# Block means of the values in the lead: value rows as weights under four streaming columns, then a turn by the identity

## The chip, the cores and the metric

The kernel runs on 1 core of one Trainium2 chip. The metric is the time of one execution on the device in microseconds, lower is better. TensorE (PE for its matmuls, PEld for its weight loads), VectorE (DVE), ScalarE (ACT), GpSimd (POOL) and the queue of the DMA issues on SyncE (SP) run side by side, each in the order of its own program.

## The reference

An attention with a band of neighbours and block summaries feeds two feed-forward layers. What matters here is the attention: each query sees the keys nearer than 16 and, for each block of 32 positions, one summary key (the maximum) and one summary value (the mean).

```python
B, H, S, D = q.shape            # 2, 8, 768, 64
block, window = (32, 16)
k_sum = k.reshape(B, H, nb, block, D).max(axis=3)
v_sum = v.reshape(B, H, nb, block, D).mean(axis=3)
scores_l = scale * np.matmul(q, k.transpose(0, 1, 3, 2))
mask_l = np.abs(pos[:, None] - pos[None, :]) < window
scores_s = scale * np.einsum('bhsd,bhnd->bhsn', q, k_sum) + np.log(block)
a = softmax(concatenate([where(mask_l, scores_l, -1e9), scores_s]))
attn = np.matmul(a, np.concatenate([v, v_sum], axis=2))
x = attn, 1536 tokens x 512
x = (relu(x @ w_in) ** 2) @ w_out             # 512 -> 2048 -> 512
x = silu(x @ w_in2) @ w_out2
```

The change touches how `v_sum` of the first batch is computed: 24 means (`NSUM`) of 32 value rows each, for all 512 columns.

## The kernel before

The 1536 tokens are worked off in 24 attention tiles of 64 queries (`QT`). A tile sees 96 neighbour positions (`NWIN`) and the 24 summaries: 120 keys (`NK`), with 4 pairs of heads (`NHP`). The first layer runs in three blocks of 512 tokens, the second layer after them. The first 8 tiles (`NLEAD`) are the lead: they must be done before the first feed-forward product `h0_0` can start. The matmuls of the layers use fp32r operands split in high and low parts; those of the attention are fp32, and each fp32 matmul stands in the trace as two records, each with a weight load of its own. The PE transposes (`psa`, `psv1`) are one record each.

For a lead tile the steps are: `psl` (scores `pss`, one pair of heads at a time, in quarters of the array), `ttl` on DVE (mask and minimum), `exl` on ACT (exponential into `T`), `ze`, `rc`, `nt` on DVE (sum, inverse, norm), `psa` on PE (L480, four transposes of T), `a` (copy to SBUF, on DVE for tiles 5, 6 and 7, else on ACT), and for two tiles together `av` (L503, products with the values), `xh` on ACT and `xl` on DVE (high and low parts of the layer's input `xt0`).

The means of the values: `share` (L376 to L397) holds a pattern of 1/32. `vs(c)` (L709) is one matmul for each 128 value rows, six in all, with a slice of `share` as weights (24 columns) and 512 value columns streaming; they add up in the PSUM tile `psv0` on partitions 96 to 119. `vmean(i)` (L713) is an ACT copy that spreads `psv0` over four tiles' value operands (`vlead`), i = 0 for tiles 0 to 3 and i = 1 for 4 to 7. `av` reads `vlead`.

What sets the order: `first_order()` (L70) lists every step of the first block with an engine, a duration, a due time and its dependencies, plays them through, and the program is recorded in the resulting order, engine by engine (L831 to L834). The engines then run in just that order. In the first block that fixes PE, DVE, ACT and the DMA issues of SP. The table's durations and due times are the author's; a due time decides between steps that are ready together. The weight chunks of the layers are decoded in the same order by ACT (`sc`: `c_wi`, `c_wo`; `hi`: `wi`, `wo`) and DVE (`sh`, `st2`, `lo`).

Of the kernel before, what the change touches and what calls it, by code (L numbers as in the profile page):

```python
# [10 lines left out]
F32 = mybir.dt.float32  # L11
# [8 lines left out]
B, H, S, D = 2, 8, 768, 64  # L20
DM, DFF = 512, 2048
NTOK = B * S
P = 128
WIN = 16
KBLK = 32
NSUM = S // KBLK
QT = 64
NWIN = QT + 2 * WIN
NK = NWIN + NSUM
TPB = S // QT  # L30
NG = B * TPB
NHP = H // 2
# [12 lines left out]
NLEAD = 8  # L45
NGRP = 4
# [3 lines left out]
PHASE = 96  # L50
# [19 lines left out]
def first_order():  # L70
# [3 lines left out]
    A, M = .15, .25  # L74
    shift = dict()

    def op(eng, name, arg, dur, due, deps=(), bank=(), kb=0):
        o = index[name, arg] = dict(eng=eng, name=name, arg=arg, dur=dur, due=due + shift.get(name, 0), deps=list(deps), bank=bank, kb=kb,
                                    n=len(ops))
        ops.append(o)  # L80
# [27 lines left out]
            op("act", "kwl", (hp, i), .5, -50 + hp + 51 * i, [("kt", hp, 0)])  # L108
            op("vec", "ksl", (hp, i), .13, -50 + hp + 48 * i, [("ksum", hp, 0)])
    for c in range(6):  # L110
        op("pe", "vs", c, .92, 2.7 + .1 * c, [("vr", c // 2, 0)])
    for i in range(NLEAD // NGRP):
        op("act", "vmean", i, 1.9, -5, [("vs", c, M) for c in range(6)] + [("vl", i, 0)] * 0)
    for i in range(NVF):
        op("act", "vfm", i, .6, tile_due(NLEAD) - 10 + i, [("vmean", 0, 0), ("xh", LEADX[-1], 0)])

# [107 lines left out]
    while todo:  # L224
# [5 lines left out]
        t, _, _, o = min(picks)  # L230
        t, _, _, o = min((p for p in picks if p[3]["eng"] == o["eng"] and p[0] <= t), key=lambda p: p[1:3])
# [13 lines left out]
def kernel(  # L245
# [17 lines left out]
    vec, act, pool, pe, sp = nc.vector, nc.scalar, nc.gpsimd, nc.tensor, nc.sync  # L263
# [10 lines left out]
    ps_h = ctx.enter_context(tc.tile_pool(name="ps_h", bufs=2, space=PSUM))  # L274
# [3 lines left out]
    def mm(o, l, r, **kw):  # L278
        pe.matmul(o, l, r, **kw)  # L279

    def copy(eng, o, i, scale=1.0):
        if eng is act:
            return act.activation(out=o, in_=i, func=AF.Copy, scale=scale)  # L283
        return eng.tensor_copy(out=o, in_=i)  # L284
# [88 lines left out]


    share_p = ctx.enter_context(tc.tile_pool(name="share_p", bufs=1, side="right"))
    share = share_p.tile([P, PHASE - 8], F32, tag="share", name="share")  # L376
    att_ctx = ExitStack()
    cp = att_ctx.enter_context(tc.tile_pool(name="cp", bufs=1, side="right"))
    p1 = att_ctx.enter_context(tc.tile_pool(name="p1", bufs=1, side="right"))
# [2 lines left out]
    first_p = first_ctx.enter_context(tc.tile_pool(name="first_p", bufs=1))  # L382

    cst_sb = cp.tile([P, 8 * LINE], F32, tag="cst", name="cst_sb")
    id_sb = cst_sb[:, 3 * NK:3 * NK + P]
# [7 lines left out]
    ksum, vsum, vsumT = {}, {}, {}  # L393

    pool.memset(share, 0.0)
    for j in range(P // KBLK):
        pool.memset(share[j * KBLK:(j + 1) * KBLK, NSUM - P // KBLK + j:NSUM - P // KBLK + j + 1], 1.0 / KBLK)  # L397
    st = {}

    def summaries(b, sums, tag):  # L400
# [234 lines left out]
    def first_block():  # L635
        x = xt[0]
        ws, kts, vrows, hs, gs, rs, cs, halves = {}, {}, {}, {}, {}, {}, {}, {}
# [1 line left out]

        idle_in = wi_p.tile([P, 512], F32R, tag="wi", name="idle_in")  # L640
        idle_out = ps_h.tile([P, 512], F32, tag="h", name="idle_out")
        psv = ps_h.tile([P, DM], F32, tag="h", name="psv0")
        vec.memset(idle_in.bitcast(F32), 0.0)
        early = first_p.tile([P, 1], F32, tag="early", name="early")
        act.activation(out=early, in_=idle_in[:, 0:1].bitcast(F32), func=AF.Exp)
# [61 lines left out]
            turn(FILL.get(ghp, 0))  # L707

        def vs(c):  # L709
            lo = NSUM - P // KBLK - c * (P // KBLK)  # L710
            mm(psv[NWIN:NK], share[:, lo:lo + NSUM], vrows[c // 2][:, c % 2], start=(c == 0), stop=(c == S // P - 1))

        def vmean(i):  # L713
            means = psv[NWIN:NK]
            copy(act, vlead[NWIN:NK, i * NGRP:i * NGRP + NGRP].rearrange("p g h d -> p g (h d)"),
                 bass.AP(means.tensor, means.offset, [means.ap[0], [0, NGRP], means.ap[1]]))

# [101 lines left out]
        def psa(g):  # L819
            for i in (g,) if g < NLEAD else (g, g + 1):  # L820
                transposes(i)

        do = dict(kt=kt, q=q, cst=cst_, vr=vr, vl=vl, ksum=ksum_, kwl=kwl, ksl=ksl, vs=vs, vmean=vmean, vfm=vfm, kv=kv, kvr=kvr,
                  vend=vend, vendc=vendc, vfc=vfc, kw=kw_load, qr=q_load, vf=v_load, kwc=k_sums, qd=side_by_side,
                  vis=vis, ttr=minima, exp=exps, ze=guard, rc=inverse, psl=psl, ttl=lambda a: minimum(*a),
                  exl=lambda a: exponential(*a), nt=lambda g: norm(g, vec),
# [2 lines left out]
                  st2=lambda xs: dec_join(name(xs), cs[xs]), scr=scr_, hi=hi, lo=lo, highs=highs, gemm1=gemm1_, relu=relu, sq=sq, gh=gh,  # L829
                  gl=gl, gemm2=gemm2_)  # L830
        steps = first_order()  # L831
        steps.remove(("gemm2", NF - 1))
        for what, arg in steps:
# [56 lines left out]
    with tc.manual_schedule(engines={e.engine for e in (vec, act, pe, sp)}):  # L890
        rest = first_block()
# [64 lines left out]
    us, vs = {}, {}  # L956
# [263 lines left out]
```

## Time and profile before

| what | value |
|---|---|
| median of 3 runs | 583.91 us (583.61 to 584.04) |
| the profiled execution's own time | 583.73 us |
| its span in the profile | 581.9 us |
| PE busy | 574.5 us, 99% |
| ACT busy | 360.1 us, 62% |
| DVE busy | 386.4 us, 66% |
| lead, up to the first record of `h` | 34.9 us |

The span counts from the first to the last instruction of the profiled execution; 1.8 us of its own time lie around it. Busy time of PE counts overlapping records once and includes the drain of a pipelined matmul; how close the records follow one another is read from the chain of waits, which gives each stretch the time until its successor could go on.

### The profile page before, as it was taken

How to read it: one execution, taken by the hardware profiler on the slowest of the kernel's cores; microseconds unless marked ns; L12 is line 12 of the kernel's file. 1: busy time of each engine (PE TensorE's matmuls, PEld its weight loads, DVE VectorE, ACT ScalarE, POOL GpSimd, SP SyncE). 2: the span in 40 equal slices, each digit the busy share in tenths (PEclk: the TensorE clock that was granted, in tenths of full speed). 3: DMA queues.
4: the chain of work that ended last, by engine and by line, in shares of the span. 5: the costliest groups of instructions: out<-in, count | busy, mean ns of one | idle time of the engine just before them, and what ended most of it. 6: DMA issues, size and time to landing. Idle time of an engine off the chain costs nothing.

```text
span 581.9 us, 9507 instructions
## 1 busy us (share of the span) xinstructions
PE 574.5 (99%) x3300; PEld 489.5 (84%) x3300; DVE 386.4 (66%) x966; ACT 360.1 (62%) x834; POOL 93.0 (16%) x101
## 2 busy tenths in 40 slices
PE   8999999999999999999999999999999999999997
PEld 6578888888888888888888889999988988889995
DVE  5999899953955765286454778666665666666641
ACT  5999878864646545376544677565555655555541
POOL 0010100102654452175332200000000000000000
PEclk9999999999999999999999999999999999999999
DMA  8999989755998879345880111242258411111002
GB/s 317 310 267 330 316 296 333 241 212 168 295 339 289 298 245 364 122 134 160 313 262 2 38 54 73 90 146 90 91 169 338 146 37 37 36 37 37 27 12 108
DMA packets 42240, 104.42 MB, mean 179 GB/s; under 512 B 4560, under 2 KB 11856, under 8 KB 42192
## 3 DMA queue, kind: packets, MB, share of 16 engines
q1 hardware_dynamic: 42192, 103.81, 52.7%
q8 instruction: 26, 0.43, 0.3%
q14 instruction: 22, 0.18, 0.1%
HBM read 78.37 MB, written 25.43 MB: 178 GB/s over the span
## 4 chain that ended last, share of the span: by engine, by line
PE 96%; ACT 2%; DMA 1%; DVE 1%; SPq 0%; issue 0%; DVEq 0%
PE acc L279 45%; PE h L279 23%; PE hx L279 12%; PE hz L279 6%; PE pss L279 3%; PE hy L279 3%; PE psa L483 2%; PE av L279 1%; DMA t_ksum<-in_kT_dram 1%; PE psv L279 1%; ACT vlead L283 1%; ACT T L446 0%; ACT xt L283 0%; PE idle_out L279 0%; DVE ksum L684 0%; DVE T L441 0%
## 5 line engine op out<-in xcount | busy, mean ns | idle before, releaser
L279 PE MATMUL h<-xt,wi 128*128 128x512 f32 x576 | 139.8, 392 | 1.0 <-ACT xt L283 1.0
L279 PE MATMUL acc<-g,wo 128*128 128x512 f32 x576 | 139.5, 391 | 0.0
L279 PE MATMUL acc<-wq,g 128*128 128x512 f32 x576 | 134.3, 390 | 0.0
L279 PEld LDWEIGHTS h<-xt,wi 128*128 128x128 f32 x576 | 107.1, 188 | 23.9 <-ACT xt L283 1.1
L279 PEld LDWEIGHTS acc<-g,wo 128*128 128x128 f32 x576 | 107.6, 188 | 22.6 <-issue 0.5
L279 PEld LDWEIGHTS acc<-wq,g 128*128 128x128 f32 x576 | 107.8, 188 | 21.9 <-DVE wq L287 0.3
L287 DVE TENSOR_TENSOR g<-r,g 128x512 fp32r<-128x512 f32 x48 | 38.8, 807 | 66.0 <-ACT g L283 40.1
L287 DVE TENSOR_TENSOR r_s<-v,r_s 128x256 fp32r<-128x256 f32 x48 | 20.3, 426 | 64.7 <-ACT r_s L283 64.7
L283 ACT ACTIVATE e<-hx 128x384 f32<-128x384 f32 x32 | 15.7, 492 | 60.4 <-PE hx L279 60.4
L446 ACT ACTIVATE T<-T,m 128x120 f32<-128x120 f32 x96 | 36.6, 382 | 7.0 <-DVE m L441 6.9
L283 ACT ACTIVATE g<-s 128x384 fp32r<-128x384 f32 x64 | 32.9, 516 | 10.5 <-DVE s L287 10.4
L279 PE MATMUL hx<-x_t,r_s 128*128 128x384 f32 x192 | 38.5, 335 | 0.0
L287 DVE TENSOR_TENSOR g<-s,g 128x384 fp32r<-128x384 f32 x64 | 35.3, 555 | 2.7 <-ACT g L283 1.1
L279 PEld LDWEIGHTS hx<-x_t,r_s 128*128 128x128 f32 x192 | 33.8, 188 | 0.3
L1032 ACT ACTIVATE s<-e 128x384 f32<-128x384 f32 x48 | 25.1, 523 | 8.4 <-DVE e L287 7.1
L284 POOL COPY qd<-qr 128x256 f32<-128x256 f32 x16 | 12.0, 767 | 111.0 <-PE pss L279 68.2
L287 POOL TENSOR_TENSOR wo<-c_wo,wo 128x512 fp32r<-128x512 f32 x16 | 25.9, 1619 | 19.2 <-ACT wo L283 18.7
L588 ACT ACTIVATE r<-h 128x512 f32<-128x512 f32 x16 | 9.6, 597 | 30.9 <-PE h L279 30.9
L592 ACT ACTIVATE r<-h 128x512 f32<-128x512 f32 x16 | 9.5, 593 | 30.6 <-PE h L279 30.6
L287 DVE TENSOR_TENSOR s<-e,s 128x384 f32<-128x384 f32 x48 | 26.4, 551 | 0.3 <-ACT s L1032 0.3
L287 POOL TENSOR_TENSOR r<-r 128x512 f32<-128x512 f32 x16 | 16.6, 1040 | 49.3 <-ACT g L593 38.1
L477 DVE TENSOR_SCALAR T<-T,r 128x120 f32<-128x120 f32 x96 | 24.2, 316 | 0.5
(112 smaller groups left out, 905.8 us busy)
## 6 DMA issues: line engine op xcount, KB each, us to landing
raw_wi<-in_w_in_dram SPq DMA_DIRECT2D x16, 512.0 KB, 5.0
raw_wo<-in_w_out_dram SPq DMA_DIRECT2D x16, 512.0 KB, 5.4
raw_wp<-in_w_out_dram SPq DMA_DIRECT2D x16, 512.0 KB, 4.9
split<-wo SPq DMA_DIRECT2D x16, 512.0 KB, 3.8
raw_wj<-in_w_in_dram SPq DMA_DIRECT2D x16, 512.0 KB, 4.7
wo<-split SPq DMA_DIRECT2D x16, 512.0 KB, 3.6
c<-scr_dram SPq DMA_DIRECT2D x32, 256.0 KB, 2.8
scr_dram<-c_wo SPq DMA_DIRECT2D x16, 256.0 KB, 3.7
```

Source lines behind the costliest of these rows:

```text
L279: pe.matmul(o, l, r, **kw)
L283: return act.activation(out=o, in_=i, func=AF.Copy, scale=scale)
L284: return eng.tensor_copy(out=o, in_=i)
L287: return eng.tensor_tensor(out=o, in0=a, in1=b, op=op)
L446: act.activation(out=d["T"][:, c], in_=d["T"][:, c], func=AF.Exp, bias=d["m"][:, c:c + 1], scale=-1.0, accum_out=d["z"][:, c:c + 1])
L477: st["norm"] = vec.tensor_scalar(out=T[:, c], in0=T[:, c], scalar1=r[:, c:c + 1], scalar2=None, op0=ALU.mult)
L483: pe.transpose(ps[0:NK, c], d["T"][:, c], id_sb)
L588: act.activation(out=r, in_=h, func=AF.Relu)
L592: act.activation(out=r, in_=h, func=AF.Relu)
L1032: act.activation(out=s, in_=src, func=AF.Sigmoid)
```

## The change

`vs(c)` becomes four matmuls, one for each pair of heads: the value rows (128 x 128) are now the weights, and `share`, cut to four columns, streams. Each writes four columns of `psv0`, which now holds the means with value columns on the partitions (128 x 4 x 24). Nothing is accumulated over c any more. A new DVE step `vsc` copies `psv0` to SBUF (`vsumT0`), a new PE step `vst` turns it by four fp32 matmuls with the identity into a new PSUM tile `pst0` (24 rows on partitions 96 to 119, 512 columns), and `vmean` reads `pst0`. The planner gets other durations and due times for these steps, `vs` earlier and the two `vmean` with due times of their own, and so it moves others.

```diff
     for c in range(6):
-        op("pe", "vs", c, .92, 2.7 + .1 * c, [("vr", c // 2, 0)])
-    for i in range(NLEAD // NGRP):
-        op("act", "vmean", i, 1.9, -5, [("vs", c, M) for c in range(6)] + [("vl", i, 0)] * 0)
+        op("pe", "vs", c, .47, 1.4 + .1 * c, [("vr", c // 2, 0)])
+    op("vec", "vsc", 0, .3, 1.4 + .7, [("vs", c, M) for c in range(6)])
+    op("pe", "vst", 0, .9, 1.4 + .7, [("vsc", 0, A)])
+    op("act", "vmean", 0, 1.9, 0.9, [("vst", 0, M)])
+    op("act", "vmean", 1, 1.9, 1.8, [("vst", 0, M)])
...
-    share = share_p.tile([P, PHASE - 8], F32, tag="share", name="share")
+    share = share_p.tile([P, PHASE - 8], F32, tag="share", name="share")[:, 0:P // KBLK]
...
-        pool.memset(share[j * KBLK:(j + 1) * KBLK, NSUM - P // KBLK + j:NSUM - P // KBLK + j + 1], 1.0 / KBLK)
+        pool.memset(share[j * KBLK:(j + 1) * KBLK, j:j + 1], 1.0 / KBLK)
...
-        psv = ps_h.tile([P, DM], F32, tag="h", name="psv0")
+        psv = ps_h.tile([P, NHP, NSUM], F32, tag="h", name="psv0")
...
         def vs(c):
-            lo = NSUM - P // KBLK - c * (P // KBLK)
-            mm(psv[NWIN:NK], share[:, lo:lo + NSUM], vrows[c // 2][:, c % 2], start=(c == 0), stop=(c == S // P - 1))
+            n = P // KBLK
+            for hp in range(NHP):
+                mm(psv[:, hp, c * n:(c + 1) * n], vrows[c // 2][:, c % 2, hp * P:(hp + 1) * P], share, start=True, stop=True)
+
+        def vsc(_):
+            vsumT[0] = first_p.tile([P, NHP, NSUM], F32, tag="vsumT0", name="vsumT0")
+            copy(vec, vsumT[0], psv)
+
+        def vst(_):
+            ps = st["vst"] = ps_h.tile([P, NHP, P], F32, tag="h", name="pst0")
+            for hp in range(NHP):
+                mm(ps[NWIN:NK, hp], vsumT[0][:, hp], id_sb, start=True, stop=True)
 
         def vmean(i):
-            means = psv[NWIN:NK]
+            means = st["vst"][NWIN:NK].rearrange("p c d -> p (c d)")
```

The order moves at three places of the lead. In the rows below, the name before the arrow is written, those behind it are read; the number at a tile's name is its attention tile, the one behind the underscore only its place in memory. A row counts matmuls, not records.

TensorE, from the first transposes of the lead on, before:

```order
L483 MATMUL psa0_345<-cst_sb_105,T0_142 120x128 x4
L279 MATMUL pss4_312<-kws1_1_141,qrlead1_111 64x120 x2
L279 MATMUL pss5_325<-kws1_1_141,qrlead1_111 64x120 x2
L483 MATMUL psa1_364<-cst_sb_105,T1_147 120x128 x4
L279 MATMUL pss6_340<-kws1_0_140,qrlead1_111 64x120 x2
L279 MATMUL pss6_340<-kws1_1_141,qrlead1_111 64x120 x4
L483 MATMUL psa2_387<-cst_sb_105,T2_152 120x128 x4
L279 MATMUL pss7_401<-kws1_0_140,qrlead1_111 64x120 x4
L279 MATMUL pss7_401<-kws1_1_141,qrlead1_111 64x120 x2
L483 MATMUL psa3_410<-cst_sb_105,T3_157 120x128 x4
```

and now:

```order
L281 MATMUL psv0_124<-share_92,vrows0_197 128x4 x4
L485 MATMUL psa0_348<-cst_sb_105,T0_142 120x128 x4
L281 MATMUL pss4_312<-kws1_1_141,qrlead1_111 64x120 x2
L281 MATMUL pss5_325<-kws1_1_141,qrlead1_111 64x120 x2
L485 MATMUL psa1_368<-cst_sb_105,T1_147 120x128 x4
L281 MATMUL psv0_124<-share_92,vrows0_197 128x4 x4
L281 MATMUL pss6_385<-kws1_0_140,qrlead1_111 64x120 x2
L485 MATMUL psa2_390<-cst_sb_105,T2_152 120x128 x4
L281 MATMUL pss6_385<-kws1_0_140,qrlead1_111 64x120 x2
L281 MATMUL pss6_385<-kws1_1_141,qrlead1_111 64x120 x2
L485 MATMUL psa3_408<-cst_sb_105,T3_157 120x128 x4
```

The first two groups of the new products (c = 0 and 1) stand here, and the scores of tiles 6 and 7 move back behind them.

TensorE, from there to the products with the values, before:

```order
L279 MATMUL pss7_401<-kws1_1_141,qrlead1_111 64x120 x2
L279 MATMUL psv0_124<-vrows0_197,share_92 24x512 x2
L483 MATMUL psa4_441<-cst_sb_105,T4_162 120x128 x4
L279 MATMUL psv0_124<-vrows1_199,share_92 24x512
L483 MATMUL psa5_459<-cst_sb_105,T5_167 120x128 x4
L279 MATMUL psv0_124<-vrows1_199,share_92 24x512
L279 MATMUL psv0_124<-vrows2_201,share_92 24x512 x2
L483 MATMUL psa6_487<-cst_sb_105,T6_172 120x128 x4
L483 MATMUL psa7_499<-cst_sb_105,T7_177 120x128 x4
L279 MATMUL av0_507<-a0_143,vlead_112 64x64 x8
```

and now:

```order
L281 MATMUL pss6_385<-kws1_1_141,qrlead1_111 64x120 x2
L281 MATMUL psv0_124<-share_92,vrows1_199 128x4 x8
L281 MATMUL pss7_440<-kws1_0_140,qrlead1_111 64x120 x4
L281 MATMUL pss7_440<-kws1_1_141,qrlead1_111 64x120 x2
L485 MATMUL psa4_451<-cst_sb_105,T4_162 120x128 x4
L281 MATMUL pss7_440<-kws1_1_141,qrlead1_111 64x120 x2
L281 MATMUL psv0_124<-share_92,vrows2_201 128x4 x8
L485 MATMUL psa5_480<-cst_sb_105,T5_167 120x128 x4
L281 MATMUL pst0_491<-cst_sb_105,vsumT0_486 24x128 x4
L485 MATMUL psa6_510<-cst_sb_105,T6_172 120x128 x4
L281 MATMUL av0_516<-a0_143,vlead_112 64x64 x8
```

The last value products stand ahead of `psa5` and the turn behind it; `psa7` has moved behind the first two `av`.

ScalarE, around the copies of the means (`vlead`), before:

```order
L283 ACTIVATE a4_163<-psa4_441 120x512
L326 ACTIVATE c_wi0_457<-raw_wi0_207 128x512
L446 ACTIVATE T6_172,z6_175<-T6_172,m6_174 128x120 x2
L446 ACTIVATE T7_177,z7_180<-T7_177,m7_179 128x120
L283 ACTIVATE wi0_474<-c_wi0_457 128x512
L446 ACTIVATE T7_177,z7_180<-T7_177,m7_179 128x120 x3
L283 ACTIVATE vlead_112<-psv0_124 24x2048 x2
L283 ACTIVATE xt0_88<-av0_507 128x4x128
```

and now:

```order
L285 ACTIVATE a4_163<-psa4_451 120x512
L328 ACTIVATE c_wi0_478<-raw_wi0_207 128x512
L448 ACTIVATE T6_172,z6_175<-T6_172,m6_174 128x120 x2
L448 ACTIVATE T7_177,z7_180<-T7_177,m7_179 128x120
L285 ACTIVATE wi0_500<-c_wi0_478 128x512
L285 ACTIVATE vlead_112<-pst0_491 24x2048
L448 ACTIVATE T7_177,z7_180<-T7_177,m7_179 128x120 x3
L285 ACTIVATE vlead_112<-pst0_491 24x2048
L285 ACTIVATE xt0_88<-av0_516 128x4x128
```

The last three exponentials of tile 7 now stand between the two copies.

Behind the lead, the planner also moves steps of the first block, on all engines and in the DMA queue: the products with the values of tiles 8 and 9 (`av8`) and the scores of tiles 10 and 11 come three layer groups earlier on PE, and the decoding steps of ACT and DVE follow. The loads of the lead keep their order.

## Rows read from the trace of the kernel before

**Rows 1.** The page: engines' busy time, and the granted clock in 40 slices
```profile
PE 574.5 (99%) x3300; PEld 489.5 (84%) x3300; DVE 386.4 (66%) x966; ACT 360.1 (62%) x834; POOL 93.0 (16%) x101
...
PEclk9999999999999999999999999999999999999999
```
**Rows 2.** Stage table: length, busy of PE, PEld, DVE, ACT, POOL, clock, DMA
```profile
34.90:128.00 93.10, 93.09 (x629) 76.92 (x629) 82.64 (x248) 79.10 (x182) 6.25 (x8) 1.00 0.86 290
```
**Rows 3.** Chain of waits, end of the lead: start us, us until the successor, what
```profile
17.35 0.58 PE psa L483 x4
...
19.43 0.91 PE pss L279 x12
...
21.35 1.83 PE psv L279 x4
...
23.76 0.97 PE psv L279 x2
...
25.31 2.70 PE psv L279 x6
...
28.04 3.63 ACT vlead L283 x2
...
31.70 0.60 ACT xt L283
...
32.88 0.98 ACT xt L283 x2
33.86 0.51 ACT wi L283
34.36 0.50 ACT xt L283
...
34.91 5.74 PE h L279 x24
```
**Rows 4.** Chain of waits, like operations in the first block
```profile
40.64 1.79 PE pss L279 x32
...
65.38 1.08 PE av L279 x32
...
108.80 0.44 PE psv L737 x4
```
**Rows 5.** Weight loads that begin up to 34.95, then up to 35.05 us
```profile
34.90 0.19 PEld L279 LDWEIGHTS h<-xt,wi 128*128 128x128 f32 x1 [1.13 <-ACT xt L283]
...
34.90 0.30 PEld L279 LDWEIGHTS h<-xt,wi 128*128 128x128 f32 x2 [1.13 <-ACT xt L283]
```
**Rows 6.** Weight loads of a transpose, up to 15.82, then 15.90 us
```profile
15.79 0.14 PEld L483 LDWEIGHTS psa<-cst_sb,T 128*120 128x120 f32 x1
...
15.79 0.19 PEld L483 LDWEIGHTS psa<-cst_sb,T 128*120 128x120 f32 x2
```
**Rows 7.** Weight loads of av, two halves of the array, up to 30.00, 30.05 us
```profile
29.96 0.14 PEld L279 LDWEIGHTS av<-a,vlead 120*64 120x64 f32 x2 [0.50 <-ACT vlead L283]
...
29.96 0.20 PEld L279 LDWEIGHTS av<-a,vlead 120*64 120x64 f32 x4 [0.50 <-ACT vlead L283]
```
**Rows 8.** ScalarE in order of time: start us, us, what
```profile
23.80 0.60 ACT L283 ACTIVATE a<-psa 120x512 f32<-120x512 f32 x1 [0.24 <-PE psa L483]
24.29 0.68 ACT L326 ACTIVATE c_wi<-raw_wi 128x512 f32<-128x512 f32 x1
24.88 0.38 ACT L446 ACTIVATE T<-T,m 128x120 f32<-128x120 f32 x1
...
26.01 0.61 ACT L283 ACTIVATE wi<-c_wi 128x512 fp32r<-128x512 f32 x1
...
28.04 3.63 ACT L283 ACTIVATE vlead<-psv 24x2048 f32<-24x2048 f32 x2 [0.28 <-PE psv L279]
```
**Rows 9.** VectorE in order of time
```profile
15.98 0.21 DVE L284 COPY kws<-ksum 128x96 f32<-128x96 f32 x1
...
28.41 0.86 DVE L477 TENSOR_SCALAR T<-T,r 128x120 f32<-128x120 f32 x4
```

More of the change, by code (lines that the diff above doesn't have):

```diff
@@ L821, in psa @@
                 transposes(i)
-        do = dict(kt=kt, q=q, cst=cst_, vr=vr, vl=vl, ksum=ksum_, kwl=kwl, ksl=ksl, vs=vs, vmean=vmean, vfm=vfm, kv=kv, kvr=kvr,
+        do = dict(kt=kt, q=q, cst=cst_, vr=vr, vl=vl, ksum=ksum_, kwl=kwl, ksl=ksl, vs=vs, vsc=vsc, vst=vst, vmean=vmean, vfm=vfm, kv=kv, kvr=kvr,
                   vend=vend, vendc=vendc, vfc=vfc, kw=kw_load, qr=q_load, vf=v_load, kwc=k_sums, qd=side_by_side,
```

## The prediction

> **What bounds the kernel now.** I read the page first. PE is busy for 99% of the span, and its granted clock shows 9 in every slice, full speed (2.4 GHz) [rows 1]. So time is won or lost only where PE waits, or where its own stream gets longer. The stage table says where that is not: from 34.90 to 128.00 us PE is busy for 93.09 of 93.10 us [rows 2], and the chain of waits stays on PE from there to the end but for the last output. The first feed-forward product, `h` at 34.91 us, is the start of a dense stream; whatever moves that start moves the end by as much, unless a new hole opens behind it.
>
> The chain of waits shows what holds the start [rows 3]. From 17.35 to 28.01 us it runs on PE without a break: transposes `psa`, scores `pss` and the old value sums `psv`, whose three rows are 1.83 + 0.97 + 2.70 = 5.50 us for 12 records. Then it passes to ACT: two copies of the means, 3.63 us from 28.04, and the four `xt` copies with two decoding steps between them, to 34.86. The reader should see that PE is the limit ahead of 28.01 and ACT behind it, and that `psv` is last on PE and the means first on ACT: any delay of the means goes straight into `h`.
>
> The decisive question is what a weight load costs where hardly anything streams. The trace has three kinds that begin on a waiting PE. For `h`, one load stands in a stretch of 0.19 us, two in 0.30: the second begins 0.11 us after the first, for 128 columns, though the first product had nothing ahead of it [rows 5]. For `av`, 64 columns, each half of the array starts its second load 0.06 us on [rows 7]. For the transposes, 120 columns, it is 0.05 us [rows 6]. So loads of fp32 and fp32r operands take about 0.86 ns a column, and those of transposes about half.
>
> **The change, part by part.**
>
> *Removed:* 5.50 us of `psv` on PE.
>
> *Added, value products:* six groups of four fp32 matmuls of two records each are 48 records, each with a load of 128 columns of fp32. Four streaming columns hide nothing of the next load, so a record takes the load's 0.11 us: 48 x 0.11 = 5.28 us. From below, at the transposes' rate [rows 6], it would be 0.057 us a record and 2.74 us in all; from above, with nothing overlapped, the full 0.19 us of a load [rows 5] and 9.12 us. I take 0.11, as these are plain fp32 loads of just that width. [...]
>
> *Added, returns to quarters:* the full-array products now break up the scores. Before, PE went back from full-array work to quarters four times in the lead, now six times. A return costs what remains when steady records are taken away: three pairs of scores take 0.91 us [rows 3], and 12 records at 1.79/32 [rows 4] are 0.67, which leaves 0.24; a `psa` takes 0.58 and four turning records 0.44 [rows 4], which leaves 0.14. Together 0.38, twice 0.76 us. From below nothing.
>
> So `psa5`, by which all scores and value products must be through, ends at 28.01 - 5.50 + 5.28 + 0.76 = 28.55 us.
>
> *Added, `vsc`:* a DVE copy of 128x96. The like copy takes 0.21 us [rows 9]. It waits for the last value product, which stands one `psa` (0.58) ahead of that point, so it is hidden.
>
> *Added, `vst`:* eight records with 128 streaming columns. At the scores' rate, two halves at once, 2 x 1.79/32 = 0.112 for 120 columns, so 0.12 each: 0.96 us, 28.55 to 29.51. From below 0.11 [rows 4], 0.88.
>
> *Moved on ACT:* the first copy waits for `vst` and, a handover of some 0.04 us on, runs 29.55 to 31.37 (3.63/2 each). ACT waits idle before it: `a4` needs `psa4`, at about 25.9 (28.55 less `psa5`, 0.58, sixteen value records, 1.76, and one pair of scores with its change of form, some 0.3), and behind `a4` (0.49) stand only 0.59, twice 0.38, 0.38 and 0.61 us of work [rows 8], to about 28.7. `wi` also waits for a DVE step that stands behind `vsc`; that may bring it close to 29.5, not past it by more than tenths. The three exponentials that were done before (three times 0.38, 1.15 us [rows 8]) come now, to 32.5, then the second copy, to 34.35.
>
> *End of the lead:* `av4` and `av6` need that copy, 2 x 1.08 us [rows 4] and a change of array form, 36.6 us; the last `xt` copy is 0.50, so `h` begins at 37.1 to 37.2. `psa7` needs the norm of tile 7, 0.86 us [rows 9] and some tenths of small steps behind 32.5, then its own 0.58: 34.4, just in time. The decoding step `wi` that stood between the copies, 0.51, has gone behind the last one; it buys nothing, since `av6` is later than ACT.
>
> The sum: `h` at 37.15 against 34.91 us, **2.2 us later**.
>
> *Moved behind the lead:* `av8` and `pss10` come three layer groups earlier. Only one group, 2.7 us, is left between `psa9` and `av8` for two `a` copies (0.5 each) behind two steps of the layer (0.6 each) on ACT; it covers them with a microsecond to spare, and a late start of PE gives every other engine and every DMA 2.2 us more. I put this at nothing; if the cover failed, PE would wait some tenths. The loads of the lead keep their order on SP, and POOL only writes a smaller `share`.
>
> The profiled execution took 583.73 us, 0.18 below the median of 583.91. 583.73 + 2.2 = **585.9 us**. Without the returns and with the shorter `vst` it is 1.4 later (585.1); with 0.125 a record and dearer returns 3.1 (586.8).
>
> **Rivals.**
>
> *Fast loads (not slower).* If a load of value rows runs at the transposes' rate [rows 6], the value products take 2.74 us and `vmean` starts 2.54 earlier than in my sum, at 27.0: `h` 0.3 us earlier than now. Even free products would not give more than 0.7: ACT alone, without those three exponentials, is through at 28.04 - 0.28 - 1.15 = 26.6 [rows 8], and that is 2.95 before 29.55. So 583.0 to 583.4, no change that can be measured. It decides at about 0.063 us a record, where the delay vanishes. For it: transposes show that the array can take a load of this size in half the time. Against it: `h` and `av` do not, and both are fp32 kinds. [...] No run here shows a product of four columns.
>
> *Nothing overlaps.* If each of the small records waits for its whole load, 9.12 us, `h` comes 3.84 us later again: 589.8 us. For it, the 0.19 that a load shows; against it the 0.11 between two loads [rows 5].
>
> *Faster than ACT's limit.* For over 0.2%, the first block would have to lose time that it does not show now; 93.09 of 93.10 us leave none [rows 2].
>
> That the change does nothing can be left out: PE's order shows it.
>
> **How the numbers follow.** About 0.2%, 1.17 us, is what a measurement of this kernel can tell from no change. My sum has 0.72, of which 0.08 lies under 1.17 us; fast loads 0.18; no overlap 0.05; faster 0.05. That makes slower 0.64 + 0.05 = 0.69, the same 0.18 + 0.08 = 0.26, faster 0.05. The likeliest case alone runs from 585.1 to 586.8. The range reaches down to the fast loads, 583.1, and up to 587.2 for products of 0.13 us a record; it leaves out the case without overlap and what lies beyond ACT's limit.
>
> **What would show it.** In the profile after, each group of eight value records should take 0.88 us on the chain and the pitch of their loads should be 0.11; `vst` about 1 us near 28.6; the first `vlead` copy near 29.5 with ACT idle for it to wait on PE; the `xt` copies up to 37; `h` at 37.1; and PE dense from there on, as now. Records at 0.06 would make me wrong at the load price. A first copy that starts on time with `h` still late would put the fault at my reading of `av6`; a hole behind `h`, or a granted clock that falls in the stretch of loads, would be a cost that I have not put in.

## The result and the profile after

The changed kernel takes 590.25 us in the median of four executions (588.72 to 591.14), the kernel before 583.80 beside it (583.61 to 584.04): 1.0108 times as long, 95% interval 1.0086 to 1.0129. Forecast were 585.9 us and a range up to 587.2. The sign was right, the time 4.35 us too low. The profiled execution took 590.0 us, 6.27 more than that of before.

The page of the changed kernel, busy time and granted clock in 40 slices (against [rows 1]):

```profile
PE 580.6 (99%) x3344; PEld 498.4 (85%) x3344; DVE 385.5 (66%) x967; ACT 360.5 (61%) x834; POOL 95.3 (16%) x101
...
PEclk9789999999999999999999999999999999999999
```

Before, every digit of the clock was a 9. Now the second and third slice, 14.7 to 44.1 us, are low. The stage table says what lies there (against [rows 2]: length, busy time of PE, PEld, DVE, ACT, POOL, granted clock, DMA share and GB/s):

```profile
11.66:23.13 11.47, 11.47 (x127) 10.36 (x127) 9.97 (x78) 10.21 (x44) 0.00 (x0) 1.00 1.06 281
23.13:33.37 10.24, 10.14 (x54) 8.12 (x53) 5.78 (x28) 4.17 (x16) 0.00 (x0) 0.50 1.04 329
33.37:40.92 7.55, 5.54 (x136) 4.71 (x136) 5.61 (x15) 7.47 (x14) 1.48 (x2) 1.00 0.32 96
40.92:128.00 87.08, 87.08 (x572) 72.02 (x573) 82.28 (x246) 76.72 (x179) 6.73 (x8) 1.00 0.89 305
```

For 10.24 us TensorE was granted half its clock (0.50), though the profile has it busy for 10.14 of them; before and behind it had all of it (1.00). (Below, such a stretch is called a fall, and 1.00 the full clock.) From the first `h` on it is dense again.

The traces give the clock only as this share. What the forecast and the expectations call 2.4 GHz is 1.00, their 1.2 GHz is 0.50. At 1.00, in the kernel before, 12 records of `h`, 512 columns each, take 2.72 us and six of `hx`, 384 each, take 1.04 (chain); so a column costs an estimated 0.417 ns, 2.4 columns a ns:

```profile
45.42 2.72 PE h L279 x12
...
327.60 1.04 PE hx L279 x6
```

The chain of waits of the changed kernel gives the prices on both sides of the drop (start us, us until the successor, what; against [rows 3]):

```profile
15.38 0.98 PE psv L281 x8
...
16.86 0.67 PE pss L281 x8
17.53 0.58 PE psa L485 x4
18.11 0.79 PE psv L281 x8
18.90 0.43 PE pss L281 x4
...
21.60 2.08 PE psv L281 x16
23.68 1.40 PE pss L281 x12
25.09 1.04 PE psa L485 x4
26.13 0.61 PE pss L281 x4
26.73 3.50 PE psv L281 x16
30.23 0.95 PE psa L485 x4
31.18 1.85 PE pst L281 x8
33.05 1.87 ACT vlead L285
34.95 1.24 ACT T L448 x6
36.22 1.87 ACT vlead L285
...
40.92 5.74 PE h L281 x24
```

The reader should see three things. A value record costs 0.10 to 0.12 us at a granted clock of 1.00 (0.79/8, 0.98/8), and 3.50/16 = 0.219 at 0.50. Everything else in the slow stretch is dearer too: a `psa` 1.04 and 0.95 for 0.58 [rows 3], twelve scores 1.40 for 0.91. And `h` begins 40.92 - 34.91 = 6.01 us later than before, of which I had forecast 2.2. Of the 6.27 us all but 0.26 lie ahead of `h`.

ScalarE and, in the last row, VectorE around the turn (start us, us, what, in brackets the idle time ahead and what ended it):

```profile
26.16 0.60 ACT L285 ACTIVATE a<-psa 120x512 f32<-120x512 f32 x1 [2.10 <-PE psa L485]
...
31.16 0.63 ACT L285 ACTIVATE wi<-c_wi 128x512 fp32r<-128x512 f32 x1 [2.71 <-DVE c_wi L336]
33.05 1.87 ACT L285 ACTIVATE vlead<-pst 24x2048 f32<-24x2048 f32 x1 [1.26 <-PE pst L281]
```
```profile
30.27 0.26 DVE L286 COPY vsumT<-psv 128x96 f32<-128x96 f32 x1 [2.71 <-PE psv L281]
```

ScalarE stood idle for 2.10 + 2.71 + 1.26 us, in the end for PE each time. Not all of that is the clock: in wide88 below, at full clock, ScalarE waits 1.02 us ahead of the same `a` and 1.26 ahead of the same `wi`. The queue behind `vsc` is there as forecast: the copy waits for the last product, `c_wi` stands behind it on VectorE, and `wi` waits on ScalarE for that.

### The profile page after: what moved, and what is told of

It is laid out like the page before. It is cut to its first block, busy times and chain, and to the rows that moved or that the text cites. A ratio compares the mean times of both kernels' runs of the same rounds, so it can differ in the third digit from the quotient of the medians.

```text
span 588.2 us, 9600 instructions
## 1 busy us (share of the span) xinstructions
PE 580.6 (99%) x3344; PEld 498.4 (85%) x3344; DVE 385.5 (66%) x967; ACT 360.5 (61%) x834; POOL 95.3 (16%) x101
## 4 chain that ended last, share of the span: by engine, by line
PE 98%; ACT 1%; DVE 0%; issue 0%; DVEq 0%
PE acc L281 45%; PE h L281 23%; PE hx L281 11%; PE hz L281 6%; PE pss L281 4%; PE hy L281 3%; PE psa L485 2%; PE av L281 1%; PE psv L281 1%; PE idle_out L281 1%; ACT vlead L285 1%; ACT xt L285 0%; PE pst L281 0%; ACT T L448 0%; DVE ro L286 0%
```

## The experiments

The theory, called clock theory: the price of a record was right, but PE lost half its clock in the stretch of small products, and its work there took up to twice as long. The rivals: the loads themselves, whatever streams; the new order; the order of ScalarE.

**Same loads, more columns** (wide88). The pattern tile is 88 columns wide anyway, 84 of them zeros; a later group overwrites the zeros that an earlier one wrote.

```diff
-    share = share_p.tile([P, PHASE - 8], F32, tag="share", name="share")[:, 0:P // KBLK]
+    share = share_p.tile([P, PHASE - 8], F32, tag="share", name="share")
...
-                mm(psv[:, hp, c * n:(c + 1) * n], vrows[c // 2][:, c % 2, hp * P:(hp + 1) * P], share, start=True, stop=True)
+                mm(psv[:, hp, c * n:c * n + PHASE - 8], vrows[c // 2][:, c % 2, hp * P:(hp + 1) * P], share, start=True, stop=True)
```

> Same loads, same order, same number of records as the changed kernel; only each value product streams 88 columns (four of the pattern, 84 of zeros) instead of four. Clock theory (the value rows are loaded at the price that I forecast, 0.11 us a record, but a PE that mostly loads and hardly streams is granted 1.2 GHz): the granted clock stays at 2.4 GHz through the lead, sixteen value records take about 2.0 us instead of 3.50, the turn about 1.0 instead of 1.85, h begins near 37 instead of 40.92 and the time is 586 to 587; up to 588 if 88 columns do not fit beside a load. Rival, loads: it is the loads of 128 columns one after another that lower the clock or cost 0.2 us each, whatever streams: h stays near 41 or later, 590 to 592.

586.98 us against 584.21 of before on the same chip, ratio 1.005 (1.0036 to 1.0065). In the profiled execution, the slowest of the four (588.09), the clock was low once, early, and full over the value products (chain, then stage table):

```profile
23.45 1.95 PE psv L281 x16
25.39 0.93 PE pss L281 x12
...
27.60 1.96 PE psv L281 x16
```
```profile
11.48:14.90 3.42, 3.42 (x26) 2.68 (x26) 2.39 (x12) 2.10 (x7) 0.00 (x0) 0.50 1.06 364
14.90:40.00 25.10, 22.63 (x298) 19.47 (x295) 20.95 (x110) 21.53 (x68) 1.24 (x2) 1.00 0.86 247
```

That early stretch puts all behind it some 1.5 us later (the first value products begin at 17.15 us, in wide88_exps_first at 15.61), so that `h` begins at 39.01 here. 84 more streaming columns bring a record from 0.115 to 0.121 us (48 in 5.54 and in 5.82), and the products keep a granted clock of 1.00. More work on PE, over 3 us less time: the same 48 loads alone did not lower the clock here.

**Idle products between** (fill6): `turn(1)` at the end of `vs(c)`.

> The changed kernel with one idle product of 512 streaming columns behind each of the six groups of value products (0.23 us each, 1.4 us in all). Clock theory: the granted clock stays at 2.4 GHz, the rows between 23.68 and 33.03 us, 9.35 us in the changed kernel, fall to about 5.4, and h begins near 38.3 instead of 40.92: 587 to 587.6, so added work makes it faster. Rival, loads or order: the same rows stay and 1.4 us come on top, 591 to 592.

589.05 us (588.13 to 591.06), above what I expected (an idle product takes 0.34 us on the chain at full clock, where I had 0.23), but the four executions tell it apart among themselves: 588.13 and 588.66 with a mean granted clock of 1.00, 589.44 with 0.993, 591.06 with 0.99. In the last, the profiled one, the fall begins at 25.09 us, where the changed kernel's began at 23.13 in one profile and, as shown further down, at 25.47 in another:

```profile
25.09:35.33 10.24, 9.82 (x44) 7.62 (x42) 5.82 (x25) 4.15 (x10) 1.21 (x2) 0.50 0.99 334
```

So with six idle products two of four executions keep the clock; that these products also put the fall off is not shown. The same program is 0.8 to 2.9 us faster where it keeps the clock.

**Old products, new order** (order_only): `vs` as before the change, `vsc` and `vst` empty, `vmean` from `psv0`, the planner's table as changed.

> The value sums by the products of the kernel before (24 columns as weights, 512 streaming, no copy and no turn), in the order of the changed kernel. Clock theory: full clock throughout, h about 1 us later than the 34.91 of the kernel before (two more returns to quarters 0.76, three exponentials between the two copies of the means 1.15, less psa7 off the path), 584.3 to 585.3. Rival, order: the new order itself delays the lead by most of what was seen, 588 to 590.

586.29 us (585.33 to 587.77), 1 us above what I expected. Two of five executions had a clock of 0.996; the three others stand at 585.33, 585.59 and 586.29. In the profiled one (585.33, mean clock 0.999, the fastest) `h` begins 1.32 us later than before:

```profile
28.20 1.88 ACT vlead L285
...
36.23 5.74 PE h L281 x24
```

The order costs something of its own, 1.1 to 2.1 us at a mean clock of 0.999 or 1.00, where I had put 1 on returns and exponentials, but not 6.

**New products, old order** (old_due): `vs` with .92 and 2.7 as before, the other new steps and both copies with a due time of -5.

> The new value products and the turn, but with the due times of the kernel before, so that the scores come first, the value products late and closer together, and both copies of the means in one piece. Clock theory: the granted clock falls again, somewhat later, and the cost is alike, 588 to 591. Rival, order: without the new order most of the loss goes, 585 to 586.5.

589.71 us (589.25 to 590.23), as the clock theory has it. The fall comes in the old order too, with the products late and close together:

```profile
23.68:33.92 10.24, 10.24 (x49) 9.21 (x49) 6.23 (x22) 4.20 (x16) 0.00 (x0) 0.50 1.04 330
```

Next, at full clock, the terms of my sum. **Exponentials first** (wide88_exps_first): the due time of the first `vmean` is 1.8 instead of 0.9.

> As wide88 (88 streaming columns, so that the clock stays up), but both copies of the means get the due time 1.8, so that ScalarE does the last three exponentials of tile 7 ahead of the first copy, in a time when it waits anyway, and both copies in one piece. Theory, order of ScalarE: of what wide88 has over the kernel before, the three exponentials between the copies are 1.2 us; h comes 1.0 to 1.3 us earlier than in wide88, 585.7 to 586.0 against its 586.98. Rival, hidden: the second copy has slack or the first copy starts later by as much, no difference from wide88.

586.61 against 583.92, 2.69 over before, where wide88 was 2.77 over: no difference, and my theory falls. The chain says why; with it `pst` and a row of sixteen weight loads from the timelines, and the stage in which the changed kernel had its fall:

```profile
28.23 0.69 DVE c_wi L336
...
28.95 0.63 ACT wi L285
29.58 1.13 ACT T L448 x6
...
30.73 3.64 ACT vlead L285 x2
...
37.61 5.73 PE h L281 x24
```
```profile
28.38 1.05 PE L281 MATMUL pst<-cst_sb,vsumT 128*24 128x128 f32 x8
```
```profile
26.00 1.86 PEld L281 LDWEIGHTS psv<-share,vrows 128*128 128x128 f32 x16
```
```profile
23.13:33.37 10.24, 8.37 (x87) 6.84 (x88) 8.34 (x38) 7.94 (x25) 0.00 (x0) 1.00 1.05 333
```

The exponentials stand behind `wi`, which waits for `c_wi` behind `vsc`. They did not move into idle time: the first copy only starts 1.15 us behind the end of `wi`, and from the start of `wi` to `h` it is 8.66 us, in wide88 8.53.

**Fewer products** (wide88_one): only the group c = 0; the means are then incomplete.

> As wide88, but only the products of the first 128 value rows are done (8 records instead of 48), the other five sixths of the value sums are left out. Theory, PE holds the means: 40 records at 0.122 us are 4.9 us less on PE; ScalarE and the exponentials between the copies keep part of it, so h comes 2 to 3.5 us earlier than in wide88, 583.5 to 585. Rival, the products are not what holds the means (ScalarE's or VectorE's order is): less than 1 us earlier, 586 to 587.

584.42 us in ten executions, 583.2 to 586.43. Those with a clock of 1.00 lie from 583.2 to 584.18, no better than the 583.92 of before; one with 0.996 took 584.67, and four with 0.991 to 0.993 lie from 585.0 to 586.43. `h` began at 34.72 us in the profiled one. So PE's products are on the path of wide88, and yet taking 40 of 48 away gains nothing on the old kernel. Its chain runs over VectorE's norms and ScalarE (`wi`, then the first copy at 26.84 us), where I had worked out for the rival of fast loads that ScalarE could not begin the copies before 26.6: that rival would have won next to nothing either.

**Products twice** (wide88_twice): `for hp in [0, 1, 2, 3] * 2`.

> As wide88, but every value product is issued twice (96 records instead of 48). Theory, a record costs its load: 48 more at 0.122 us, all on the path, 5.9 us: 592.5 to 593.2, h 5.9 us later than in wide88. Rival, a record can hide beside others: under 4 us more, below 591.

593.14 us (592.27 to 593.71), 9.22 over before; less the 2.77 of wide88 that is 6.45, 0.6 more than I had put on the records. The 96 records take 1.95 + 1.75 + 3.73 + 3.75 = 11.18 us on the chain, 0.116 each, close to the 0.111 us at which loads follow one another (shown further down); none of them hides. The rest is not fully accounted for; three of its four executions have a clock of 0.996 or 0.997, the profiled one with a fall of 3.41 us from 37.53, behind the products.

**No products on PE** (pool_sums).

```diff
-        op("pe", "vs", c, .47, 1.4 + .1 * c, [("vr", c // 2, 0)])
+        op("pool", "vs", c, 3.2, -5, [("vr", c, 0)])
...
+            while n > 1:
+                tt(pool, t[:, :, 0:n], t[:, :, 0:n], t[:, :, n:2 * n], ALU.add)
+                n //= 2
```

> A version without value products on PE: the values are loaded with positions along the free axis, GpSimd adds them up by halves (15 additions, 3.2 us estimated for each third from its additions in the first block), four transposes turn the sums, and both copies of the means follow in one piece, scaled by 1/32. Theory, ScalarE is the next limit: PE loses 5.5 us of products and gains 0.44 us of transposes, but ScalarE's own work is not less, so h comes 0.3 to 0.9 us earlier than the 34.91 us of the kernel before, 583.3 to 583.9 against its 584.2. Rival, clock: PE, without the products, stands idle in the lead, is granted 1.2 GHz for a while, and the version is slower than the kernel before, 585 to 588. Rival, GpSimd: its additions slow VectorE or end after 26 us, 585 or more at full clock.

590.22 us (589.41 to 592.1); the theory fell, and the costs that both rivals name are in it, though no run shows that a PE without work lowered the clock. The granted clock was at 0.50 twice, and while GpSimd added, four norms on VectorE took 3.22 us where they take 0.86 [rows 9] (timelines of POOL and DVE):

```profile
13.32 7.03 POOL L288 TENSOR_TENSOR vrows<-vrows 128x512 f32<-128x512 f32 x9 [11.72 <-DMA vrows<-in_vT_dram]
```
```profile
15.81 3.22 DVE L478 TENSOR_SCALAR T<-T,r 128x120 f32<-128x120 f32 x4
```
```profile
20.27:23.68 3.41, 3.41 (x24) 2.52 (x22) 3.41 (x23) 1.88 (x9) 1.58 (x7) 0.50 1.07 244
...
30.51:37.34 6.83, 4.43 (x46) 3.46 (x48) 6.20 (x19) 5.77 (x11) 1.25 (x2) 0.50 0.85 230
```

In the same execution the norms are back at 0.86 us at 27.91, in a stretch in which GpSimd does nothing (0.00 us busy from 23.68 to 30.51). At 33.20 two of them take 1.20 us on the chain, in the last stretch above, in which GpSimd is busy for 1.25. What one engine does to the other is not shown beyond these times.

Last, on one chip, the changed kernel once more, a mixture, and what is left of the idea. **The changed kernel again** (changed_again):

> The changed kernel itself once more, beside the two others and the kernel before on one chip. Clock theory: a stretch at 1.2 GHz that begins between 21 and 26 us in every profiled execution, h near 41, 589 to 591. Rival, chance: the clock falls in some executions only, and the time has two levels some 3 us apart, 586.5 and 590.

589.53 us against 584.13 (589.19 to 591.07), every execution with a clock of 0.988 to 0.993: not a matter of chance. Here the fall came behind the third and fourth group, which so show their price at full clock (chain, the weight loads of these sixteen records, then stage):

```profile
22.29 1.88 PE psv L281 x16
...
26.55 3.50 PE psv L281 x16
```
```profile
22.21 1.86 PEld L281 LDWEIGHTS psv<-share,vrows 128*128 128x128 f32 x16
```
```profile
25.47:39.12 13.65, 12.62 (x106) 10.43 (x104) 8.18 (x32) 9.10 (x20) 1.22 (x2) 0.50 0.81 267
```

Sixteen loads in 1.86 us, of which the last takes 0.19, begin 0.111 us apart, and the row of wide88_exps_first, with 88 columns, is just as long.

**Four columns in the last two groups only** (mixed): `w = PHASE - 8 if c < 4 else n`.

> The changed kernel with 88 streaming columns in the first four groups of value products and four columns in the last two only (16 records, behind the scores of tile 7, and followed by psa5 and the turn). Clock theory, many loads together: one such stretch is not enough, the clock stays up, 586.5 to 587.3. Rival, any stretch: the clock falls within or behind the last two groups, later than in the changed kernel, and a part of the 3.4 us that wide88 won is lost again, 588 to 589.5.

587.95 us (586.2 to 588.54), between the two: two of five executions kept a clock of 1.00 (586.2 and 587.32), the others 0.993 to 0.997. In the profiled one the last two groups ran at full clock (1.00 from 11.66 to 28.90 us), and the clock fell behind them, during the turn:

```profile
26.01 1.89 PE psv L281 x16
```
```profile
28.90:35.73 6.83, 5.93 (x75) 4.91 (x73) 4.98 (x17) 6.47 (x11) 1.52 (x2) 0.50 0.93 278
```

Three of five executions with a lower clock, against two of eight in wide88 and wide88_exps_first together (0.996 and 0.997): that the one stretch of sixteen is enough in some executions fits this, but so few executions do not show it.

**What is left of the idea** (wide88_old_tr): wide88 with the due times of old_due, and `pe.transpose(ps[0:NSUM, hp], vsumT[0][:, hp], id_sb)` in `vst`.

> What is left of the idea when every cost found so far is taken off: 88 streaming columns, the due times of the kernel before (four returns to quarters instead of six, both copies in one piece, no exponentials between them), and the turn by four transposes instead of eight fp32 records. Theory: value products 5.86 us instead of 5.50, psa6 (0.58) and the transposes (0.44) ahead of the first copy: h 1.4 us later than the 34.91 us of the kernel before, 585.1 to 585.6. Rival, more of the sum was order than I think: within 0.5 us of the kernel before.

585.05 us against 584.13 in eleven executions, ratio 1.0016 (1.0007 to 1.0025), at the lower end of what I expected. `h` comes 0.94 us later than before:

```profile
28.12 0.18 DVE vsumT L286
...
28.34 0.62 PE pst L723 x4
...
28.99 3.63 ACT vlead L285 x2
...
35.85 5.73 PE h L281 x24
```

It takes back most of the loss and still does not beat the kernel before. None of the versions does.

## Why the prediction was wrong, step by step

- **psv removed, 5.50; 48 records at 0.11, 5.28.** Right. At a granted clock of 1.00 the groups take 0.98 + 0.79 (changed kernel), 1.88 (its second profile) and 1.89 (mixed), 5.54 us or 0.115 each, and within a row the loads begin 0.111 us apart. The transposes' 0.057 is out, and so is the upper bound: a load lasts 0.19 us, but the next begins before its end.
- **Returns, vsc, vst.** Right at full clock: eight and four scores behind a return take 0.67 and 0.43 us, 0.2 more than 0.056 a record [rows 4], and the `psa` behind them 0.58, so that a return costs some 0.36 where I had 0.38; with 88 columns the turn stands at 28.38 for 1.05 us, where I had 28.55 and 0.96; `vsc` is hidden behind `psa5`; `wi` ends at 29.58, where I said close to 29.5.
- **Both copies, av, h at 37.15.** Nearly right at full clock: 37.61 with the exponentials first, 0.28 of it for the wider products (5.82 against 5.54). In the changed kernel 40.92.
- **PE dense behind h.** Right: 87.08 of 87.08 us to 128.
- **The step that failed** is one that the sum took over unsaid from [rows 1]: "its granted clock shows 9 in every slice". I carried every price at full clock into a stretch whose work I had just replaced, and named a falling clock only as "a cost that I have not put in". What the runs show in its place: from 23.68 us to the end of the turn at 31.18 + 1.85 the changed kernel, at a granted clock of 0.50, needs 9.35 us; wide88_exps_first, at 1.00 and with the same order on PE up to the turn, from 23.86 to 28.38 + 1.05, needs 5.57. That is 3.8 us, and 6.01 - 3.8 = 2.2 us is what I had forecast. So close an agreement is partly luck: 0.2 us of the fall lie ahead of 23.68 (sixteen records in 2.08 for 1.88), and this execution reached its first value products 0.2 us earlier than wide88_exps_first (15.38 and 15.61). Whole executions give 2.7 to 3.7: the changed kernel 6.45 us over before, less 2.77 for wide88, and on the chip of the last runs 5.40, less 2.69 for wide88_exps_first.
- **The rivals.** "Nothing overlaps" gave 589.8 us, close to the result, and was wrong in its mechanism: its records of 0.19 would show in every group, and the groups ahead of the fall show 0.10 to 0.12.

Open: how the chip decides. The fall begins at 23.13, 25.47 and 23.68 us in three profiles with four columns throughout, and lasts 10.24, 13.65 and 10.24 us. Wide88 had one ahead of any value product, in the profiled execution, and wide88_twice one behind them; some executions of order_only and wide88_one show a lower mean clock as well; the 35 of the kernel before beside these runs all show 0.998 or more. Shown is that with four columns throughout, and no idle products between, every execution has it (nine of the changed kernel with a mean clock of 0.987 to 0.993, four of old_due with 0.988 to 0.991), and that with 88 columns it is gone from their stretch in four profiles (1.00 there in wide88, wide88_exps_first and wide88_twice, a mean of 0.999 in wide88_old_tr). PE had no wait ahead of the fall in the changed kernel (11.47 of 11.47 us busy); in pool_sums it was busy for only 6.75 of the 9.27 us ahead of the first one (11.00 to 20.27). What else in a changed lead brings it now and then was not tried.

## What to carry to other kernels

A matmul that hardly streams cost, in this kernel, about the distance at which weight loads follow one another, 0.115 us where the loads of 128 fp32 columns begin 0.111 apart, though one load lasts 0.19: I would count records times that, not columns. Before you carry prices from a profile into a stretch whose work you replace, ask whether the granted clock of that profile will hold there; the fall cost this kernel 3.8 us, 1.5 of them on the last sixteen value records (3.50 us for 1.96), the rest on everything around them. Look at the clock's row first when a result is too slow, and try wider streams: here they cost 0.006 us a record.

## What the hardware showed that I had not expected

- PE, busy for 10.14 of 10.24 us, was at a granted clock of 0.50 all the while. Busy time was no sign of a full clock; the profile books a value record of four columns with 0.25 us (the median of 48), though the next one starts 0.11 us later at full clock.
- 84 more streaming columns cost 0.006 us a record on average, nothing from one load to the next within a row, and gave 2.7 to 3.7 us back.
- One program has executions with and without the fall: fill6 from 588.13 to 591.06 us, wide88_one from 583.2 to 586.43. A mean clock of 0.99 in the list of runs is the sign.
- While GpSimd added, four norms on VectorE took 3.7 times as long (3.22 for 0.86 us).
